# Where the split weights of a three-part network are made: two temporary buffers against the raw tile itself

## The chip, the core and the metric

The kernel runs on one core of one Trainium2 chip, as one program. The metric is the device time of one execution in microseconds (us). Engines: PE (matrix products; PEld its weight loads), DVE (elementwise), ACT (elementwise and activations), POOL, and SP, which here only issues DMA transfers. In the trace every engine takes its instructions in the order of the program text; one that has to wait holds up those that stand behind it on that engine.

## The reference, cut to what matters

```python
ret = scale * (q @ k.T) * decay_mask            # 4 batches, 8 heads, 576 positions, 64 wide
x   = (ret @ v)  rearranged to [2304, 512]
h   = x @ w_in                                  # [2304, 2048]
x   = (h * tanh(softplus(h))) @ w_out           # "mish", back to [2304, 512]
g   = x @ w_gate; val = x @ w_val               # [2304, 1536] each
out = (g / (1 + exp(-g)) * val) @ w2_out        # "silu gate", back to [2304, 512]
```

The five weight matrices (`w_in`, `w_out`, `w_gate`, `w_val`, `w2_out`) arrive as 64-bit floats; q, k, v and the output are fp32.

## The kernel before

**Products in parts.** PE multiplies fp32r words. Each weight and each activation is split into a high part (a rounding copy, on ACT) and a low part (the fp32 word minus its high part, on DVE), and each product is made of three matrix products: high by high, high by low, low by high. A raw weight tile needs conversion first: each 64-bit word lies in it as two 32-bit halves, and `rebias_raw` (L112: an ACT scale, a DVE shift), `sign` (L117) and `join` (L121) turn each pair of halves into one fp32 word. In the kernel before the joined words lie in every second place of the raw tile ("lo"); the places between ("hi") are then free.

**Stages.** (1) Retention, to about 106 us of the trace. (2) `slot(s)` (L728), s = 4 to 63, in four blocks of sixteen: one tile of the hidden layer is made (`g1`, twelve matmuls on `h`, L664), `mish` and the split run on ACT and DVE (L715, L722, L726), and four slots later the tile goes into the four accumulators (`g2`, twelve matmuls on `acc`, L698). When a block of sixteen ends, `g2_out` (L703) copies the accumulators out, two on ACT, two on DVE, and the next block's activations are split (L364 on ACT, L369 on DVE). (3) The last third of the tokens runs by Strassen's scheme, seven products for eight: `pair1(0)` to `pair1(7)` (L954), seven products each (`te`, L883). (4) The second network by the same scheme (`strassen`, L1092, `outs2`, L1195).

**What the scheme needs of the weights.** Of each block of four sub-matrices a11, a12, a21, a22 the products use seven (`USES`, L178): a11, a12, a22 and the sums s1 = a21+a22, s3 = a11-a21, s2 = s1-a11, s4 = a12-s2. They are made once, during stages 2 and 3, stored to DRAM (`comb1`, `comb`, `combf`) and streamed back when wanted. The first network's weights (`group1(i)`, L289, eight groups) lie already split in SBUF; the second network's (`group(n)`, L219, eighteen groups of two raw tiles) are loaded, converted, summed, split and stored. Raw tiles alternate between two sets of two.

**Parts.** `cast` (L195) takes a tile from the pool `c` (two buffers, one tag) and writes the high part of a run of words into it; `lower` (L200) writes the low part beside it and issues one store for each sub-matrix on SP. A group has four such runs (of the plain words one of 512 and one of 256 columns, and two of 512 with the sums, which lie in "hi"), so every buffer is used twice in a group, and a cast waits on ACT until the stores from its buffer have landed.

**Order and pace.** The order is written out by hand. The steps of all groups stand in one list (`pieces`, L331), each with a cost; `Pace` (L340) adds an allowance at the end of every slot or product and runs as many steps as it covers. `third` (the `group1` steps) gets 3.0 in each slot from s = 20, which lasts to s = 31; `second` (the `group` steps) gets 3.1 in each of s = 32 to 50, 2.3 in s = 51 to 63 and 1.03 at each product of `pair1(1)` to `pair1(7)` (L52, L752 to 757, L1009). A group costs 8.25. The load of group n+1 stands behind the first step of group n on SP. Groups 16 and 17 are worked in stage 4 with tiles lent from the weight space (`raw_second`, `parts_second`, L1049, L1055).

Of the kernel before, what the change touches and what calls it, by code (L numbers as in the profile page):

```python
# [7 lines left out]
F32 = mybir.dt.float32  # L8
# [8 lines left out]
def retention_mish_swiglu(  # L17
# [33 lines left out]
    NC = 4  # L51
    RATES, AHEAD = (3.0, 3.1, 2.3, 1.03), 45  # L52
    EARLY = (9, 11, 14, 17)
# [36 lines left out]
    def words(j):  # L90
        w = raw[j].rearrange("p (n t) -> p n t", t=2)
        return w[:, :, 0], w[:, :, 1]
# [93 lines left out]

    def parts_first(nm, n):
        return pools["c"].tile([128, 2, n, KH], F32R, tag="c", name=nm)

# [16 lines left out]

    def put(x, dsts, nm):
        lower(x, cast(x, nm), dsts)
# [5 lines left out]
    def combine(v, names):  # L214
        for o, a, b, op in ADDS:
            if o in names:
                nc.vector.tensor_tensor(out=v[o], in0=v[a], in1=v[b], op=op)

    def group(n):  # L219
        i, z = divmod(n, 2) if n < 2 * PAIRS else (n - 2 * PAIRS, 2)  # L220
        keys = [f"{'gvf'[z]}{i}_{e}" for e in range(2)]
        v = {}

        def load():
            for e in range(2):
                src = rows(w2_out, 2 * i + e) if z == 2 else cols((w2_gate, w2_val)[z], 2 * i + e)
                raw_load(keys[e], src, z == 2, e + 2 * (n % 2))
                lo, hi = words(keys[e])
                for h in range(2):
                    r, k = (h, e) if z == 2 else (e, h)  # L230
                    v[f"a{r + 1}{k + 1}"] = lo[:, h * KH:(h + 1) * KH].bitcast(F32)
                    v["s" + "1324"[2 * e + h]] = hi[:, h * KH:(h + 1) * KH].bitcast(F32)

        def dst(nm):
            c = USES.index(nm)
            if z == 2:
                return combf[c][i // 2][:, i % 2]
            c += z * NG
            return comb[i][c // 2][:, c % 2]

        def runs():
            lo, hi = ([words(k)[w].bitcast(F32) for k in keys] for w in range(2))
            one, two = (0, 1) if z == 2 else (1, 0)
            return [
                (lo[two], ("a12", "a22") if z == 2 else ("a11", "a12")),
                (lo[one][:, :KH] if z == 2 else lo[one][:, KH:], ("a11",) if z == 2 else ("a22",)),
                (hi[0], ("s1", "s3")), (hi[1], ("s2", "s4")),
            ]

        def step(k):  # L250
            x, names = runs()[k]
            c = {}

            def first():
                c[0] = cast(x, f"c{n}_{k}")

            return first, lambda: lower(x, c[0], [dst(nm) for nm in names])

        def parts_of():
            s = [step(k) for k in range(4)]  # L260

            def add_then(nm, f):
                combine(v, (nm,))
                f()

            def both(f, g):
                f()
                g()

            return [  # L270
                lambda: add_then("s1", s[0][0]), s[0][1], lambda: add_then("s3", s[1][0]),
                lambda: both(s[1][1], s[2][0]), lambda: combine(v, ("s2",)), s[2][1],
                lambda: add_then("s4", s[3][0]), lambda: None, s[3][1],
            ]

        found = []

        def nth(k):
            if not found:
                found.extend(parts_of())  # L280
            found[k]()

        return load, [
            (0.55, lambda: rebias_raw(keys[0])), (0.55, lambda: rebias_raw(keys[1])),
            (0.7, lambda: sign(keys[0])), (0.7, lambda: join(keys[0])),
            (0.7, lambda: sign(keys[1])), (0.7, lambda: join(keys[1])),
        ] + [(t, lambda k=k: nth(k)) for k, t in enumerate((0.45, 0.7, 0.45, 0.45, 0.45, 0.7, 0.45, 0.0, 0.7))]

    def group1(i):  # L289
        v = {}  # L290

        def whole():
            x = rp.tile([128, 2 * DM], U32, tag="raw3", name=f"e{i}").bitcast(F32)
            for e in range(2):
                u = unit["in", 2 * i + e]
                for h in range(2):
                    nm = f"a{e + 1}{h + 1}"
                    if nm in USES:
                        m = i * NG + USES.index(nm)
                        nc.sync.dma_start(  # L300
                            out=comb1[m // 2][:, m % 2], in_=u[:, :, h * KH:(h + 1) * KH].bitcast(F32)
                        )
# [5 lines left out]
            v["x"] = x  # L308
            v["s1"], v["s2"], v["s3"], v["s4"] = v["a22"], v["a11"], v["a21"], v["a12"]

        c = {}

        def first(*halves):
            for k in halves:
                c[k] = cast(v["x"][:, k * DM:(k + 1) * DM], f"e{i}_{k}")

        def rest(k):
            at_ = [i * NG + USES.index(nm) for nm in (("s2", "s4"), ("s3", "s1"))[k]]
            lower(v["x"][:, k * DM:(k + 1) * DM], c[k], [comb1[m // 2][:, m % 2] for m in at_])

        def adds(k):
            combine(v, (("s2", "s4"), ("s1", "s3"))[k])
            first(k)

        return [
            (1.4, whole), (0.85, lambda: adds(1)), (0.85, lambda: adds(0)), (0.7, lambda: rest(1)), (0.7, lambda: rest(0)),
        ]
# [329 lines left out]
    with tc.manual_schedule():  # L657
# [221 lines left out]

        def product(p, w, y, begin):  # L880
            for kk in range(KT // 2):
                for a, x in ((0, 0), (0, 1), (1, 0)):
                    nc.tensor.matmul(  # L883
                        p, lhsT=w[:, a, kk * 128:(kk + 1) * 128], rhs=y[kk][:, x, :],
                        start=begin and kk == 0 and (a, x) == (0, 0), stop=kk == KT // 2 - 1 and a == 1,
                        skip_group_check=True,
                    )
# [66 lines left out]
        def pair1(i):  # L954
# [22 lines left out]
            for c, (nm, tn, begin) in enumerate(PRODUCTS):  # L977
# [3 lines left out]
                m = i * NG + c  # L981
                product(p, su["e", m // 2][:, m % 2], ys["e", c], begin)
                if m % 2:
# [68 lines left out]

        turn = [0]

        def parts_second(nm, n):  # L1055
            turn[0] += 1
            return place("out", 13 + turn[0] % 3, [128, 2, n, KH], F32R, nm)

# [33 lines left out]
        def strassen(n, i, z):  # L1092
# [30 lines left out]
            for c, (nm, tn, begin) in enumerate(PRODUCTS):  # L1123
# [3 lines left out]
                m = z * NG + c  # L1127
                product(p, su[n, "gv", i, m // 2][:, m % 2], ys[n, c], begin)
                if m % 2:
# [65 lines left out]
        def outs2(n, work):  # L1195
# [50 lines left out]
            for c, (nm, tn, begin) in enumerate(PRODUCTS):  # L1246
# [8 lines left out]
                for count, (i, m) in enumerate(at_):  # L1255
                    w, g = su[n, "f", c, i // 2][:, i % 2], gt[n, c, i]
                    for a, x in ((0, 0), (0, 1), (1, 0)):
                        nc.tensor.matmul(  # L1258
                            p[m], lhsT=g[:, x, m * 128:(m + 1) * 128], rhs=w[:, a, :],
                            start=begin and i == 0 and (a, x) == (0, 0) and not (shared and m == 1),  # L1260
                            stop=a == 1 and i == PAIRS - 1, skip_group_check=True,
                        )
# [102 lines left out]
```

## Time and profile before

| | us |
|---|---|
| median of three runs (927.26 to 927.62) | 927.3 |
| the profiled execution | 930.68 |
| its span, first to last instruction | 928.6 |
| mean granted TensorE clock of the span | 0.981 of full speed |
| PE busy / DVE busy / ACT busy | 899.0 / 640.5 / 398.4 |
| stage 2 from s = 32 on, and `pair1(0)` | 224.3 to 378.3, 378.3 to about 395 |

The profile is read in three steps: what PE waits for, since PE is busy in 97% of the span; which engine made it wait, and behind what that engine itself stood; and what a stretch without such waits costs. A row of the timeline gives start, duration, engine, line, operation, tiles, and in brackets how long the engine sat idle before it and what ended that. Busy times of PE are pipelined and run into each other, so the pace of PE is read from numbers of matmuls in a stretch.

### The profile page before, as it was taken

The numbers are of one execution on the slowest core, as the hardware profiler recorded it, in microseconds if no ns is written. First come the engines' busy times: TensorE is split into PE (matmuls) and PEld (weight loads), VectorE is DVE, ScalarE is ACT, GpSimd is POOL, SyncE is SP. The second block draws the span as 40 slices with busy tenths as digits, with TensorE's granted clock in tenths as the row PEclk, the third lists the DMA queues.
The fourth block names the chain that finished last, engine by engine and source line by source line (L and its number), as shares of the span: only waits on it lengthen the run. The fifth ranks groups of instructions, "written<-read, shape, count | busy, mean of one in ns | idle before, by whom it ended". The sixth has DMA issues, their size and how long they took to land.

```text
span 928.6 us, 16096 instructions
## 1 busy us (share of the span) xinstructions
PE 899.0 (97%) x6122; PEld 874.6 (94%) x6122; DVE 640.5 (69%) x1233; ACT 398.4 (43%) x803; POOL 52.7 (6%) x47
## 2 busy tenths in 40 slices
PE   9899999999899789899999999999999999999997
PEld 8798999999899789899999999999999999999997
DVE  3678699578666676566768588787558587566772
ACT  3677466334444454444545333245221345222260
POOL 3554200000000000000000000000000000000000
PEclk9799999999999889899999999999999999999999
DMA  9999266099776666768876689977977777977773
GB/s 216 241 249 245 69 184 191 12 305 296 227 233 196 206 215 221 240 209 273 278 246 204 224 275 343 312 239 249 315 252 247 251 243 260 299 252 255 236 248 113
DMA packets 155261, 217.50 MB, mean 234 GB/s; under 512 B 47792, under 2 KB 119216, under 8 KB 155184
## 3 DMA queue, kind: packets, MB, share of 16 engines
q1 hardware_dynamic: 153648, 215.25, 74.3%
q10 hardware_dynamic: 1536, 1.21, 0.4%
q8 instruction: 49, 0.80, 0.4%
q14 instruction: 28, 0.23, 0.1%
HBM read 164.00 MB, written 52.43 MB: 233 GB/s over the span
## 4 chain that ended last, share of the span: by engine, by line
PE 73%; DVE 11%; ACT 7%; DMA 6%; issue 2%; SPq 0%; ACTq 0%; DVEq 0%
PE t L883 24%; PE T L1258 15%; PE ea L921 7%; PE te L883 6%; PE h L664 6%; PE acc L698 5%; DMA comb<-c 3%; PE s L486 2%; PE o L567 2%; PE o L554 1%; ACT g L722 1%; DVE g L726 1%; ACT c L197 1%; ACT m L715 1%; DMA ecomb<-e 1%
## 5 line engine op out<-in xcount | busy, mean ns | idle before, releaser
L883 PE MATMUL t<-y,su 128*128 128x384 f32 x1512 | 268.6, 337 | 2.5 <-DVE u L890 2.0
L883 PEld LDWEIGHTS t<-y,su 128*128 128x128 f32 x1512 | 263.5, 188 | 5.9 <-DVE u L890 3.3
L664 PE MATMUL h<-xs,u 128*128 128x384 f32 x768 | 147.8, 342 | 4.4 <-ACT xs L364 3.2
L698 PE MATMUL acc<-g,u 128*128 128x384 f32 x720 | 137.9, 341 | 9.0 <-ACT y L708 8.6
L664 PEld LDWEIGHTS h<-xs,u 128*128 128x128 f32 x768 | 137.5, 193 | 5.6 <-ACT xs L364 3.5
L698 PEld LDWEIGHTS acc<-g,u 128*128 128x128 f32 x720 | 128.4, 192 | 10.1 <-ACT y L708 9.3
L1258 PE MATMUL T<-su,g 128*128 128x256 f32 x1134 | 135.7, 282 | 0.0
L1258 PEld LDWEIGHTS T<-su,g 128*128 128x128 f32 x1134 | 135.6, 190 | 0.0
L921 PE MATMUL ea<-ge,u 128*128 128x512 f32 (+1 forms) x384 | 76.0, 337 | 0.0
L883 PE MATMUL te<-ye,eu 128*128 128x384 f32 x336 | 69.4, 342 | 4.0 <-ACT scratch L987 4.0
L726 DVE TENSOR_TENSOR g<-m,g 128x384 fp32r<-128x384 f32 x64 | 35.6, 556 | 51.2 <-ACT g L722 50.9
L921 PEld LDWEIGHTS ea<-ge,u 128*128 128x128 f32 x384 | 62.0, 188 | 5.8
L883 PEld LDWEIGHTS te<-ye,eu 128*128 128x128 f32 x336 | 58.1, 192 | 6.3 <-ACT scratch L987 4.3
L1104 ACT ACTIVATE sg<-sg 128x384 f32<-128x384 f32 x54 | 28.4, 525 | 61.1 <-DVE sg L890 61.1
L1067 ACT CAST g<-ga 128x384 fp32r<-128x384 f32 x72 | 32.5, 516 | 44.8 <-DVE ga L1112 31.3
L1133 ACT COPY p<-t 128x384 f32<-128x384 f32 x35 | 16.6, 473 | 80.8 <-PE t L883 80.8
L1060 DVE TENSOR_TENSOR g<-ga,g 128x384 fp32r<-128x384 f32 x72 | 36.2, 550 | 10.5 <-ACT g L1067 10.5
L715 ACT ACTIVATE m<-h 128x384 f32<-128x384 f32 x64 | 31.1, 487 | 25.6 <-PE h L664 25.5
L890 DVE TENSOR_TENSOR u<-t,p 128x384 f32<-128x384 f32 x36 | 20.0, 556 | 27.0 <-PE t L883 25.1
L890 DVE TENSOR_TENSOR v<-t,p 128x384 f32<-128x384 f32 x36 | 20.0, 557 | 22.8 <-PE t L883 22.7
L197 ACT CAST c<-rawg 128x512 fp32r<-128x512 f32 (+1 forms) x24 | 14.4, 599 | 46.5 <-DMA comb<-c 28.5
L722 ACT CAST g<-m 128x384 fp32r<-128x384 f32 x64 | 32.9, 514 | 1.8
(137 smaller groups left out, 1102.2 us busy)
## 6 DMA issues: line engine op xcount, KB each, us to landing
su<-comb SPq DMA_DIRECT2D x126, 512.0 KB, 4.3
su<-fcomb SPq DMA_DIRECT2D x63, 512.0 KB, 4.2
comb<-c SPq DMA_DIRECT2D x84, 256.0 KB, 2.6
eu<-ecomb SPq DMA_DIRECT2D x28, 512.0 KB, 4.7
fcomb<-c SPq DMA_DIRECT2D x42, 256.0 KB, 3.1
raw<-in_moe_w_in_dram SPq DMA_DIRECT2D x16, 512.0 KB, 4.5
raw<-in_moe_w_out_dram SPq DMA_DIRECT2D x16, 512.0 KB, 3.9
ecomb<-e SPq DMA_DIRECT2D x32, 256.0 KB, 3.1
```

The source lines that it names most:

```text
L664: nc.tensor.matmul(ps, lhsT=u[:, a, kk * 128:(kk + 1) * 128], rhs=s[:, e, :], start=(c == 0), stop=(c == n - 1),)
L698: nc.tensor.matmul(accs[b][d][:, :T], lhsT=u[:, a, d * 128:(d + 1) * 128], rhs=g[:, e, :], start=(i == 0 and c == 0), stop=(i == F1 - 1 an ...
L715: nc.scalar.activation(w, hs.pop(s), AF.Mish)
L722: nc.scalar.copy(out=gs[s][:, 0, :], in_=ws[s])
L726: nc.vector.tensor_tensor(out=g[:, 1, :], in0=ws.pop(s), in1=g[:, 0, :].bitcast(F32), op=ALU.subtract)
L883: nc.tensor.matmul(p, lhsT=w[:, a, kk * 128:(kk + 1) * 128], rhs=y[kk][:, x, :], start=begin and kk == 0 and (a, x) == (0, 0), stop=kk == ...
L890: nc.vector.tensor_tensor(out=out_, in0=a, in1=b_, op=ALU.add)
L921: nc.tensor.matmul(o, lhsT=u[:, a, d * 128:(d + 1) * 128], rhs=y[:, :512] if r == 0 else y[:, 512:], start=f == 0 and (a, x) == (0, 0) and ...
L1060: nc.vector.tensor_tensor(out=out_, in0=a, in1=b_, op=ALU.subtract)
L1067: nc.scalar.copy(out=gt[n, c, i][:, 0], in_=x)
L1104: nc.scalar.activation(x, bank_ if part_ is None else x, AF.Silu)
L1258: nc.tensor.matmul(p[m], lhsT=g[:, x, m * 128:(m + 1) * 128], rhs=w[:, a, :], start=begin and i == 0 and (a, x) == (0, 0) and not (shared ...
```

## The change

The high and low parts of the second network's plain sub-matrices are made inside the raw tile; the sums get two tiles of their own; stores go out from there.

- `join_` writes the joined words densely into the front half of the raw tile (it read and wrote every second place before). The back half is then free.
- `cast` no longer takes a tile; it writes the high part of a run into the back half of the raw tile, and `lower` puts the low part over the words in the front. Stores of a11, a12, a22 read the raw tile.
- s1 and s3 are written into tile c0, s2 and s4 into c1 (`sums`), each with room for both parts; these two tiles have one buffer each (pool `c` had two buffers of one tag, the same space). Their high part goes beside them, the low part over them.
- The order of steps in a group is new, its cost 8.7, and the load of group n+1 stands behind its fourth step. The pace at the products of `pair1` is 1.1. In `group1` the sums also go to c0 and c1, and the casts stand one step later.
- In DRAM the second network's parts now lie low first, so `product` and the last product of `outs2` pick the parts by index.

```diff
-    RATES, AHEAD = (3.0, 3.1, 2.3, 1.03), 45
+    RATES, AHEAD = (3.0, 3.1, 2.3, 1.1), 45
...
-    def cast(x, nm):
-        c = parts(nm, x.shape[1] // KH)
-        nc.scalar.copy(out=c[:, 0], in_=x.rearrange("p (n k) -> p n k", k=KH))
-        return c
-    def lower(x, c, dsts):
-        nc.vector.tensor_tensor(
-            out=c[:, 1], in0=x.rearrange("p (n k) -> p n k", k=KH), in1=c[:, 0].bitcast(F32), op=ALU.subtract
-        )
-        for n, dst in enumerate(dsts):
-            nc.sync.dma_start(out=dst, in_=c[:, :, n].bitcast(F32))
+    def cast(hi, x):
+        nc.scalar.copy(out=hi, in_=x.bitcast(F32))
+    def lower(x, hi):
+        nc.vector.tensor_tensor(out=x, in0=x.bitcast(F32), in1=hi.bitcast(F32), op=ALU.subtract)
...
+        def join_(e):
+            lo, hi = words(keys[e])
+            nc.vector.scalar_tensor_tensor(
+                raw[keys[e]][:, :DM], hi, 3, lo, op0=ALU.logical_shift_left, op1=ALU.bitwise_or
+            )
+        def begin(k):
+            sums(v, c, k, 0, f"c{n}_{k}")
+        def lower_two():
+            lower(w[two][:, 0], w[two][:, 1])
+            for h, nm in enumerate(names):
+                out(nm, w[two][:, :, h])
+        def lower_one():
+            lower(w[one][:, 0, own], w[one][:, 1, own])
+            out(only, w[one][:, :, own])
+        def lower_sums(k):
+            lower(c[k][:, 0], c[k][:, 1])
+            for h, nm in enumerate((("s1", "s3"), ("s2", "s4"))[k]):
+                out(nm, c[k][:, :, h])
...
-        ] + [(t, lambda k=k: nth(k)) for k, t in enumerate((0.45, 0.7, 0.45, 0.45, 0.45, 0.7, 0.45, 0.0, 0.7))]
+            (0.45, lambda: both(lambda: begin(0), lambda: cast(w[two][:, 1], w[two][:, 0]), lambda: combine(v, "s1"))),
+            (0.45, lambda: combine(v, "s3")),
+            (0.45, lambda: both(lambda: begin(1), lambda: combine(v, "s2"))),
+            (0.45, lambda: both(lambda: cast(c[0][:, 1], c[0][:, 0]), lambda: combine(v, "s4"))),
+            (0.7, lower_two), (0.7, lambda: lower_sums(0)),
+            (0.45, lambda: both(lambda: cast(c[1][:, 1], c[1][:, 0]), lambda: cast(w[one][:, 1, own], w[one][:, 0, own]))),
+            (0.7, lambda: lower_sums(1)), (0.45, lower_one),
+        ]
...
-        return [
-            (1.4, whole), (0.85, lambda: adds(1)), (0.85, lambda: adds(0)), (0.7, lambda: rest(1)), (0.7, lambda: rest(0)),
-        ]
+        def begin(k):
+            sums(v, c, k, 1, f"e{i}_{k}")
+            for nm in (("s1", "s3"), ("s2", "s4"))[k]:
+                combine(v, nm)
+        def last_cast():
+            cast(c[1][:, 0], c[1][:, 1])
+            rest(0)
+        def sums2():
+            begin(1)
+            cast(c[0][:, 0], c[0][:, 1])
+        return [(1.4, whole), (0.85, lambda: begin(0)), (0.85, sums2), (0.7, last_cast), (0.7, lambda: rest(1))]
...
-            yield steps_[0]
+            yield from steps_[:4]
             if n + 1 < len(gr):
                 yield 0.0, gr[n + 1][0]
-            yield from steps_[1:]
+            yield from steps_[4:]
...
-        pools["c"] = cr.enter_context(tc.tile_pool(name="pc", bufs=2, side="right"))
+        pools["c"] = cr.enter_context(tc.tile_pool(name="pc", bufs=1, side="right"))
```

## Rows read from the trace of the kernel before

**Rows 1.** The page, part 1: busy us, share of the span, instructions
```profile
PE 899.0 (97%) x6122; PEld 874.6 (94%) x6122; DVE 640.5 (69%) x1233; ACT 398.4 (43%) x803; POOL 52.7 (6%) x47
```
**Rows 2.** Waits of PE, 105 to 620 us: total us, times, longest
```profile
PE acc L698 <- ACT y L708: 8.6, 2, 4.5
PE te L883 <- ACT scratch L987: 4.0, 1, 4.0
PE h L664 <- ACT xs L364: 3.2, 1, 3.2
PE h L664 <- DVE xs L369: 1.2, 1, 1.2
```
**Rows 3.** Windows: length, busy us (instructions) by engine, then PEclk, DMA share, GB/s
```profile
160.00:224.30 64.30, 64.30 (x372) 64.30 (x371) 44.01 (x84) 26.21 (x52) 0.00 (x0) 1.00 0.56 182
224.30:378.30 154.00, 140.97 (x771) 139.53 (x769) 106.02 (x214) 74.69 (x149) 0.00 (x0) 0.94 0.70 222
378.30:401.50 23.20, 19.18 (x97) 18.86 (x97) 9.59 (x20) 8.79 (x20) 0.00 (x0) 0.85 0.55 200
401.50:509.50 108.00, 108.00 (x621) 100.97 (x620) 77.39 (x156) 52.68 (x107) 0.00 (x0) 1.00 0.77 251
```
**Rows 4.** Timeline of ACT ahead of the waits of PE, 241 to 386 us
```profile
241.34 0.65 ACT L197 CAST c<-rawg 128x512 fp32r<-128x512 f32 x1 [4.93 <-DMA comb<-c]
241.90 0.48 ACT L715 ACTIVATE m<-h 128x384 f32<-128x384 f32 x1
...
246.86 0.85 ACT L708 COPY y<-acc 128x384 f32<-128x384 f32 x2
...
301.92 0.70 ACT L197 CAST c<-rawv 128x512 fp32r<-128x512 f32 x1 [1.23 <-DVE rawv L123]
...
302.87 0.95 ACT L364 CAST xs<-x 128x384 fp32r<-128x384 f32 x2
...
385.58 0.65 ACT L197 CAST c<-rawg 128x512 fp32r<-128x512 f32 x1 [6.94 <-DMA comb<-c]
```
**Rows 5.** Waits of ACT, 217 to 405 us
```profile
ACT c L197 <- DMA comb<-c: 47.2, 13, 6.9
```
**Rows 6.** Groups of instructions by shape, 231 to 400 us: busy, mean ns | idle before
```profile
L726 DVE TENSOR_TENSOR g<-m,g 128x384 fp32r<-128x384 f32 x32 | 17.8, 556 | 25.3 <-ACT g L722 25.1
L201 DVE TENSOR_TENSOR c<-rawg,c 128x512 fp32r<-128x512 f32 x16 | 11.0, 688 | 9.1 <-ACT c L197 9.1
L123 DVE SCALAR_TENSOR_TENSOR rawg<-rawg 128x512 uint32<-128x512 uint32 x12 | 8.3, 692 | 0.3
L217 DVE TENSOR_TENSOR rawg<-rawg 128x256 f32<-128x256 f32 x11 | 4.6, 421 | 0.1
L115 DVE TENSOR_SCALAR rawg<-rawg 128x512 uint32<-128x512 uint32 x12 | 4.5, 422 | 0.0
```
**Rows 7.** Timeline of DVE and ACT in the `group1` stretch, 179 to 227 us
```profile
179.51 0.89 DVE L217 TENSOR_TENSOR e<-e 128x256 f32<-128x256 f32 x2
...
183.29 1.46 DVE L201 TENSOR_TENSOR e<-e,e 128x512 fp32r<-128x512 f32 x2
184.78 1.29 DVE L304 TENSOR_TENSOR e<-u 128x512 f32<-128x512 f32 x2
...
226.16 1.02 DVE L369 TENSOR_TENSOR xs<-x,xs 128x384 fp32r<-128x384 f32 x2
...
187.84 0.62 ACT L197 CAST e<-e 128x512 fp32r<-128x512 f32 x1 [1.83 <-DMA ecomb<-e]
189.34 0.62 ACT L197 CAST e<-e 128x512 fp32r<-128x512 f32 x1 [0.88 <-DMA ecomb<-e]
```
**Rows 8.** Timeline of PE where s = 32 begins its `g1`
```profile
226.40 4.33 PE L664 MATMUL h<-xs,u 128*128 128x384 f32 x24
```
**Rows 9.** Tiles `rawg`, then `c`: from issue to landing
```profile
DMA to landing us min/median/max: 4.7/5.6/7.2
DMA to landing us min/median/max: 2.0/2.8/6.4
```

More of the change, by code (lines that the diff above doesn't have):

```diff
@@ L185, in raw_first, with parts_first @@
         return rp.tile([128, 2 * DM], U32, tag=f"raw{n}", name=f"raw{key}")
-    def parts_first(nm, n):
-        return pools["c"].tile([128, 2, n, KH], F32R, tag="c", name=nm)
+    def parts_first(k, nm):
+        return pools["c"].tile([128, 2, 2, KH], F32R, tag=f"c{k}", name=nm)
     def raw_load(key, src, whole, n):
@@ L192, in raw_load, with send, combine, sums @@
         nc.sync.dma_start(out=raw[key] if whole else raw[key].rearrange("p (k f) -> p k f", k=KT), in_=src)
-    def cast(x, nm):
-        c = parts(nm, x.shape[1] // KH)
-        nc.scalar.copy(out=c[:, 0], in_=x.rearrange("p (n k) -> p n k", k=KH))
-        return c
-    def lower(x, c, dsts):
-        nc.vector.tensor_tensor(
-            out=c[:, 1], in0=x.rearrange("p (n k) -> p n k", k=KH), in1=c[:, 0].bitcast(F32), op=ALU.subtract
-        )
-        for n, dst in enumerate(dsts):
-            nc.sync.dma_start(out=dst, in_=c[:, :, n].bitcast(F32))
-    def put(x, dsts, nm):
-        lower(x, cast(x, nm), dsts)
+    def cast(hi, x):
+        nc.scalar.copy(out=hi, in_=x.bitcast(F32))
+    def lower(x, hi):
+        nc.vector.tensor_tensor(out=x, in0=x.bitcast(F32), in1=hi.bitcast(F32), op=ALU.subtract)
+    def send(dst, src):
+        nc.sync.dma_start(out=dst, in_=src.bitcast(F32))
     ADDS = (("s1", "a21", "a22", ALU.add), ("s3", "a11", "a21", ALU.subtract),
             ("s2", "s1", "a11", ALU.subtract), ("s4", "a12", "s2", ALU.subtract))
[L214 to L217, printed above, removed]
+    def combine(v, nm):
+        (o, a, b, op), = [x for x in ADDS if x[0] == nm]
+        nc.vector.tensor_tensor(out=v[o].bitcast(F32), in0=v[a].bitcast(F32), in1=v[b].bitcast(F32), op=op)
+    def sums(v, c, k, low, nm):
+        c[k] = parts(k, nm)
+        for n, o in enumerate((("s1", "s3"), ("s2", "s4"))[k]):
+            v[o] = c[k][:, low, n]
     def group(n):
@@ L236, in dst, with out @@
+        def out(nm, src):
+            m = USES.index(nm)
             if z == 2:
[L237 to L243, printed above, removed]
-            return [
-                (lo[two], ("a12", "a22") if z == 2 else ("a11", "a12")),
-                (lo[one][:, :KH] if z == 2 else lo[one][:, KH:], ("a11",) if z == 2 else ("a22",)),
-                (hi[0], ("s1", "s3")), (hi[1], ("s2", "s4")),
-            ]
@@ L250, in step @@
[L250 to L263, printed above, removed]
-                f()
[L266 to L281, printed above, removed]
+                dst = combf[m][i // 2][:, i % 2]
+            else:
+                m += z * NG
+                dst = comb[i][m // 2][:, m % 2]
+            send(dst, src)
+        two, one = (1, 0) if z == 2 else (0, 1)
+        names = ("a12", "a22") if z == 2 else ("a11", "a12")
+        own, only = (0, "a11") if z == 2 else (1, "a22")
+        def join_(e):
[3 more added lines that the diff above has]
+            )
@@ L307, in whole @@
                 )
[L308 to L315, printed above, removed]
-        def rest(k):
[L318 to L325, printed above, removed]
-            (1.4, whole), (0.85, lambda: adds(1)), (0.85, lambda: adds(0)), (0.7, lambda: rest(1)), (0.7, lambda: rest(0)),
-        ]
+        def begin(k):
+            sums(v, c, k, 1, f"e{i}_{k}")
+            for nm in (("s1", "s3"), ("s2", "s4"))[k]:
+                combine(v, nm)
+        def rest(k):
+            lower(c[k][:, 1], c[k][:, 0])
+            for h, nm in enumerate((("s1", "s3"), ("s2", "s4"))[k]):
+                m = i * NG + USES.index(nm)
+                send(comb1[m // 2][:, m % 2], c[k][:, :, h])
+        def last_cast():
[5 more added lines that the diff above has]
+        return [(1.4, whole), (0.85, lambda: begin(0)), (0.85, sums2), (0.7, last_cast), (0.7, lambda: rest(1))]
     FIRST = 4
@@ L878, in retention_mish_swiglu, with product @@
         )
-        def product(p, w, y, begin):
+        def product(p, w, high, y, begin):
             for kk in range(KT // 2):
@@ L1051, in raw_second, with parts_second @@
             return place("in", 9, shape, U32, name) if n % 2 else pools["rx"].tile(shape, U32, tag="rx", name=name)
[L1053 to L1057, printed above, removed]
+        def parts_second(k, nm):
+            return place("out", 13 + k, [128, 2, 2, KH], F32R, nm)
         def sub(out_, a, b_):
```

29 lines of the change are left out of this document (13 added, 16 removed).

## The prediction

> **What bounds the kernel now.** The first view is the busy line of the page: PE is busy in 97% of the span, so only time that PE loses can be won [rows 1]. The second is the list of what PE waited for after retention: four kinds of wait, 17.0 us, nearly all released by ACT [rows 2]. The third asks what these waits cost together, and reads PE's pace by stretch: 372 matmuls in 64.30 us without a wait are 0.173 us each; the 771 of the next stretch should then take 133.3 us and took 154.0, the 97 after them 16.8 and took 23.2 [rows 3]. The loss is 20.7 + 6.4 = 27.1 us. It is more than the 17.0 us of the waits because the granted clock falls to a mean of 0.94 and 0.85 there: after a wait PE runs for a while at half speed, 1.2 instead of 2.4 GHz, which adds 0.6 us to every us waited. The fourth view, the timeline of ACT, tells why ACT was late: ahead of the first wait stands a cast that sat 4.93 us until a store from its buffer had landed, and `mish` and the copies of the accumulators stand behind it; ahead of the last one the same with 6.94 us [rows 4]. Such waits sum to 47.2 us, thirteen of them [rows 5]. Most cost nothing, since a hidden tile is wanted only four slots after its `mish`; those just before a block ends do. From 401.5 us on PE loses next to nothing, so everything that can be won lies between 224 and 401 us.
>
> **The change part by part.**
> *Taken away: the wait of ACT for stores.* In the new order no cast writes a place from which a store of the same group still reads. The back half of a raw tile is free since the load; c0 and c1 are stored once in a group, and their next writer comes ten steps later, at least 5.5 units of cost, 7.4 us at 3.1 units in a slot of 24 x 0.173 = 4.15 us, where a store needs 2.8 us and at most 6.4 [rows 9]. The whole 27.1 us are open to be won; what is late next decides how much of it.
>
> *What is late next in the slots: DVE.* The number of instructions stays: two shifts (0.42), two signs and two joins (0.69), four sums (0.42), three lower parts of 512 columns (0.69) and one of 256 (0.42): 7.8 us in a group, 0.89 us a unit [rows 6]. A slot then takes 3.1 x 0.89 + 0.56 for the low part of `g` = 3.3 us of DVE out of 4.15. So DVE recovers 0.8 us a slot when it is late, and ACT, with less to do, waits for it within a slot (a cast for its sums) without carrying this into the next. At the three block ends and at `pair1(0)`, what PE wants then has 2 us and more of slack if ACT and DVE are on time: copies of the accumulators are wanted 2.1 us after `g2` ends, the split activations 5 us after `g1` ends for some 3 us of work (`mish` 0.48, two copies 0.95, low parts 0.56 each) [rows 4, 6]. The second wait of PE had also a cast behind a join before it, 1.23 us [rows 4]; this is of DVE and stays, within that slack. I put 0.8 us for block ends, between 0 and 6 (two of the old waits back).
>
> *Dense words.* Whether sums and casts read every second word or neighbours: strided sums took 421 ns, dense ones 0.89 us a pair [rows 6, 7]. Nothing.
>
> *Moved: the load of the next group, and the release of raw tiles.* SP isn't paced by slots, so the place behind step four matters little; but the load of the second raw tile now waits until the store of `lower_one` has landed, where it waited for DVE before, and the first stores of the next group and the streams stand behind it on SP. From `lower_one`: 0.5 for the issue, 2.8 for the store, 5.6 for the load, at most 6.4 and 7.2 [rows 9]: 8.9 us, at worst 14. The rebias that wants it stands 9.8 units on, 13.1 us, and ACT reaches it 1 to 2 us ahead of DVE. So it is hidden by 2 us at the medians; without that cover ACT waits at a rebias as it did at a cast. 0.4 us, between 0 and 4. Streams are asked for six tiles ahead and lose nothing.
>
> *`group1`: a new loop through one buffer.* Here the writer of c0 is a sum on DVE, and one buffer is all there is. From the end of a lower part to the cast that its stores held up, the trace has 3.9 and 4.6 us (two lower parts end at 184.0 and 184.75, the casts go at 187.84 and 189.34) [rows 7]. The loop is this, two pairs of sums at 0.89 and a lower part of 0.69: 6.4 to 7.1 us, where the pace asks for a group every 4.5 / 3.0 slots = 6.2 us. So DVE falls behind by 0.1 to 0.8 us a group; it is busy for 44.0 of 64.3 us in this stretch, and part of the waiting falls into that idle time [rows 3]. Followed through s = 20 to 31 with 4.2 us, the low parts of the next block's activations start at 227.7 instead of 226.16 us [rows 7]. PE wants the first seven matmuls into its `g1`, at 226.40 + 7 x 0.173 = 227.6 [rows 8], and gets it at 228.2: 0.6 us lost, with clock 1.0. With 3.9 it is 0, with 4.6 about 4 and with clock 6.4. I take 1.0, as both durations occur and the shorter one held at the first group and later again.
> The Trainium skill, "SBUF — State Buffer", section "The DMA setup-cost knee", gives a transfer about 2 us and its bytes over 436 GB/s: 2.6 us for 256 KB, as an estimate. By it the loop would take 5.7 us, DVE would not fall behind, and the time would be 1.0 us less; the rows above are of this very transfer, with its queue and two stores in a row, and they decide.
>
> *The longer list.* A group costs 8.7 units instead of 8.25 and the slots' allowance stays (88.8), so at 1.1 a product the list ends at (139.2 - 88.8) / 1.1 = the 46th of 49 products instead of the 42nd. From product 45 of `pair1` on (counted from `pair1(0)`) two more instructions of 0.55 run at each product: the two lists overlap for eight products instead of four. DVE then has about 1.0 + 1.1 + 0.6 = 2.7 us in the 2.2 us of a product (108 us for 49) [rows 3] and is late by some 2 to 3 us at the end, just below what the 18 matmuls (3.1 us) between the end of one product and the next into the same accumulator leave. 0.5 us, between 0 and 2. Three products without pieces follow before stage 4, which starts with idle DVE. Groups 16 and 17 keep their places; nothing there.
>
> *The sum.* 27.1 won, less 0.8 + 0.4 + 1.0 + 0.5 = 2.7, net 24.4 us. On the profiled execution: span 928.6 to 904.2, its time 930.68 to 906.3. The median of the runs is 3.4 us below that execution; 927.3 - 24.4 = 903 us. With all costs at 0 it is 900, with all at their upper ends (18.4) 918.6.
>
> **The rivals.**
> *A. As summed:* 903, 900 to 907.
> *B. `group1` runs at the pace of its stores.* With 4.6 us throughout, 6.4 us are lost at s = 32, and the same lateness costs about 2 again at the copies four slots later, with the other costs 1.7: 27.1 - 10.1 = 17.0, 910. For it: 4.6 was seen in the same slot as 3.9. Against: 3.9 is seen too, and PE passes s = 32 today without a wait [rows 8].
> *C. The waits change their name.* ACT stands at the casts of c0 for the sums on DVE, just ahead of a block end, as 1.23 us did at the second wait; half of the loss stays, 13.5 us: 914. Against: DVE has 0.8 us a slot to spare.
> *D. The change doesn't do what it says:* a tile is tracked as a whole, casts into the back half wait for stores of the front, and the 47.2 us of waits return: 927.
> *E. Slower: the raw tile's loop.* Store, load, conversion and `lower_one` of one set of raw tiles run round once in two groups, 2 x 2.81 slots = 23.3 us. By medians the round takes 3.3 + 6.1 + 8.9 (7.8 and two low parts of `g`) = 18.3, by the longest rows 23.5. Above 23.3 the excess goes into ACT's wait at every rebias. To eat 27.1 us in ten groups it has to reach 28.7, that is store and load at nearly twice their medians throughout; then 930 and more. Fourteen stores of 256 KB and four loads of 512 KB in 23.3 us are 250 GB/s; `group1` moves seven such stores in 6.2 us, nearly 300, with stores of 3.9 to 4.6 us, which speaks against it.
>
> **How the numbers follow.** A 0.62, B 0.17, C 0.11, D 0.04, E 0.06. The likeliest is A: 903. From 899 to 913 lie A, B and a third of C, 0.82. A measurement of this kernel can tell about 0.2% from no change: faster 0.90 (A, B, C), the same 0.04 (D), slower 0.06 (E).
>
> **What would show it.** Right: no wait of ACT for a store between 217 and 401 us; the waits of PE for ACT's copies, for its activations and for `pair1(0)` gone, each below 1 us; the granted clock at 1.00 in the slots; about 134 us from s = 32 to `pair1(0)`. Wait rows of DVE for stores in `group1`, about 1 us each, are part of A; beyond 2 us each they speak for B. A rebias that waits for the load of its raw tile speaks for E, casts that wait over 2 us for DVE at a block end for C. I would be wrong if PE finds something else to wait for between 224 and 401 us that today stands in the shadow of ACT.

## The result, and the profile after

The changed kernel takes 899.95 us (median of four, 899.81 to 901.78), the kernel before 927.46 beside it (927.26 to 928.44): the ratio is 0.9706, with an interval of 0.9689 to 0.9723. 903 was forecast. The profiled execution of after took 901.78 us, with a span of 900.0. Two disturbed executions further down, one of `slow_27` (the one with its trace, at a mean granted clock of 0.753) and one of `slow_255`, are counted in the medians and not in the ratios.

The first view is again the page, and now says less than before: PE is busy for 99% where it was 97% [rows 1]. The second row is the granted clock in 40 slices, in tenths.

```profile
PE 888.9 (99%) x6122; PEld 866.5 (96%) x6122; DVE 639.8 (71%) x1233; ACT 396.3 (44%) x803; POOL 52.5 (6%) x47
...
PEclk9799999999999999999999999999999999999999
```

The waits of PE after retention, 105 to 620 us (total us, times, longest), answer to [rows 2]. None of the four kinds is left; what remains sums to 2.0 us, and none of it is for the slots' copies or activations.

```profile
PE t L878 <- DVE u L885: 1.0, 2, 0.6
PE acc L693 <- DVE u L134: 0.3, 1, 0.3
PE o L549 <- DVE x L575: 0.3, 1, 0.3
PE t L878 <- ACT p L1125: 0.2, 1, 0.2
PE t L878 <- DVE v L885: 0.2, 1, 0.2
```

The windows (length, busy us and instructions of PE, PEld, DVE, ACT, POOL, then PEclk, DMA share, GB/s) answer to [rows 3]. The same slots, s = 32 to 63, that took 154.0 us with 771 matmuls now take 133.2 with 768, at clock 1.00; `pair1` follows without a loss.

```profile
160.00:224.30 64.30, 64.30 (x373) 64.30 (x372) 44.59 (x86) 27.63 (x54) 0.00 (x0) 1.00 0.55 177
224.30:357.50 133.20, 133.20 (x768) 133.20 (x768) 101.70 (x204) 71.08 (x145) 0.00 (x0) 1.00 0.79 253
357.50:372.00 14.50, 14.50 (x85) 14.50 (x85) 8.13 (x18) 6.69 (x15) 0.00 (x0) 1.00 0.74 246
372.00:482.00 110.00, 110.00 (x631) 103.05 (x630) 81.24 (x165) 54.15 (x110) 0.00 (x0) 1.00 0.79 257
```

Of the waits of the other engines, 160 to 405 us, three rows matter. The 47.2 us that ACT stood for stores [rows 5] have no row any more. ACT waits for sums on DVE instead, 13.0 us in nine pieces, which costs PE nothing; the sums of `group1` wait for stores, and once a raw tile comes 0.8 us late.

```profile
ACT c L196 <- DVE c L209: 13.0, 9, 3.2
...
DVE e L209 <- DMA ecomb<-e: 10.0, 13, 3.0
...
ACT rawg L114 <- DMA rawg<-in_moe_w_gate_dram: 0.8, 1, 0.8
```

ACT at the end of the first block answers to [rows 4], where a cast sat 4.93 us and the copies of the accumulators went at 246.86. They now go at 241.72, just as PE's `g2` has ended, and PE takes the next `g2` at 243.29 without a wait.

```profile
241.72 0.85 ACT L703 COPY y<-acc 128x384 f32<-128x384 f32 x2
```

### The profile page after: what moved, and what is told of

Its sections match the earlier page's. It is cut to its first block, busy times and chain, and to the rows that moved or that the text cites. A ratio compares the mean times of both kernels' runs of the same rounds, so it can differ in the third digit from the quotient of the medians.

```text
span 900.0 us, 16088 instructions
## 1 busy us (share of the span) xinstructions
PE 888.9 (99%) x6122; PEld 866.5 (96%) x6122; DVE 639.8 (71%) x1233; ACT 396.3 (44%) x803; POOL 52.5 (6%) x47
## 4 chain that ended last, share of the span: by engine, by line
PE 92%; DVE 5%; ACT 1%; DMA 1%; issue 0%; SPq 0%; ACTq 0%; DVEq 0%
PE t L878 25%; PE T L1250 15%; PE h L659 14%; PE acc L693 13%; PE ea L916 7%; PE te L878 7%; PE s L481 2%; PE o L562 2%; PE o L549 2%; PE tk L465 1%; PE acc L891 1%; PE state L525 1%; DMA raw<-in_moe_w_in_dram 1%; PE idle L607 1%; PE tq L434 1%; DVE cv L885 1%
## 5 line engine op out<-in xcount | busy, mean ns | idle before, releaser
L659 PE MATMUL h<-xs,u 128*128 128x384 f32 x768 | 143.8, 336 | 0.0
L693 PE MATMUL acc<-g,u 128*128 128x384 f32 x720 | 134.6, 336 | 0.3 <-DVE u L134 0.3
L659 PEld LDWEIGHTS h<-xs,u 128*128 128x128 f32 x768 | 133.9, 188 | 0.4
L693 PEld LDWEIGHTS acc<-g,u 128*128 128x128 f32 x720 | 125.8, 188 | 0.6 <-DVE u L134 0.6
L721 DVE TENSOR_TENSOR g<-m,g 128x384 fp32r<-128x384 f32 x64 | 35.6, 556 | 47.2 <-ACT g L717 46.8
L1125 ACT COPY p<-t 128x384 f32<-128x384 f32 x35 | 16.5, 473 | 80.7 <-PE t L878 80.7
L885 DVE TENSOR_TENSOR u<-t,p 128x384 f32<-128x384 f32 x36 | 20.0, 556 | 28.3 <-PE t L878 27.2
L196 ACT CAST c<-c 128x512 fp32r<-128x512 f32 x36 | 22.2, 619 | 13.4 <-DVE c L209 13.4
```

Of the source, the lines that this page charges most:

```text
L659: nc.tensor.matmul(ps, lhsT=u[:, a, kk * 128:(kk + 1) * 128], rhs=s[:, e, :], start=(c == 0), stop=(c == n - 1),)
L693: nc.tensor.matmul(accs[b][d][:, :T], lhsT=u[:, a, d * 128:(d + 1) * 128], rhs=g[:, e, :], start=(i == 0 and c == 0), stop=(i == F1 - 1 an ...
L721: nc.vector.tensor_tensor(out=g[:, 1, :], in0=ws.pop(s), in1=g[:, 0, :].bitcast(F32), op=ALU.subtract)
L885: nc.vector.tensor_tensor(out=out_, in0=a, in1=b_, op=ALU.add)
```

## The experiments

Each kernel was run beside the kernel before; a ratio is against that. The theory at first was the prediction's: the gain is the waits of ACT for stores from two rotating buffers, and of these only the ones just ahead of a block end cost anything. Its rivals were the dense words, the new order and pace, and later the pace of before alone.

### Dense words alone

`dense_only` is the kernel before with the joined words in the front half of the raw tile and the sums in its back half; buffers, order and pace are the old ones.

```diff
-            lo, hi = words(keys[e])
+            lo, hi = raw[keys[e]][:, :DM], raw[keys[e]][:, DM:]
...
-            (0.7, lambda: sign(keys[0])), (0.7, lambda: join(keys[0])),
+            (0.7, lambda: sign(keys[0])), (0.7, lambda: join_(0)),
```

> The kernel before with one thing of the change alone: the joined words are written densely into the front half of the raw tile and the sums lie in the back half; parts still go through the two rotating c tiles, in the old order and at the old pace. Theory (ACT's waits for stores from c are the whole gain): ACT still waits some 45 to 50 us for comb stores between 217 and 405 us, PE still loses about 27 us, time 925 to 929 us. Rival (dense words make sums, casts and low parts cheaper, which is what helped): DVE and ACT groups shorter by 50 ns or more each, time below 915 us.

Measured: 926.76 us, ratio 0.9991 (0.9976 to 1.0006). ACT's waits for stores are as before, 47.1 us in twelve, and so are PE's: 6.7, 5.1, 4.2 and 2.0 us. Dense words bring nothing.

### The new order and pace, without working in place

`order_only` is the changed kernel with all four runs of a group through two rotating buffers of one tag again; the order, the cost of a group, the place of the load and the pace are the new ones.

```diff
-            (0.45, lambda: both(lambda: begin(0), lambda: cast(w[two][:, 1], w[two][:, 0]), lambda: combine(v, "s1"))),
+            (0.45, lambda: both(lambda: up("two", w[two][:, 0]), lambda: combine(v, "s1"))),
...
-        pools["c"] = cr.enter_context(tc.tile_pool(name="pc", bufs=1, side="right"))
+        pools["c"] = cr.enter_context(tc.tile_pool(name="pc", bufs=2, side="right"))
```

> The changed kernel with its in-place parts undone: the new order of steps, the new cost of a group, the place of the load, the new pace and the dense words stay, but high and low parts of all four runs go through two rotating c tiles again (one tag, two buffers) and the sums lie in the back half of the raw tiles. Theory: the casts of s2/s4 and of the single sub-matrix must wait for stores issued two steps earlier, so ACT waits 3 to 4 us in each group, 35 to 45 us in all, and PE loses part of it at the block ends: 908 to 930 us. Rival (the new order and pace put the steps where they do no harm): 899 to 903 us whatever ACT waits.

Measured: 930.35 us, ratio 1.0038 (1.0022 to 1.0054). The waits for stores are back under new names (217 to 405 us):

```profile
ACT c_s L196 <- DMA comb<-c_two: 39.6, 10, 5.6
ACT c_one L196 <- DMA comb<-c_s: 12.5, 10, 3.4
```

and PE waits 18.4 us in its six largest kinds (105 to 640 us), for the accumulators, the activations and `pair1(0)` as before. So order and pace alone are not the gain. It needs the writes that no store holds up.

### The load late in the list

`late_load` is the changed kernel with the load of group n+1 behind step 12 of group n instead of step 4. It takes away the cover under which the prediction costed that load at 0.4 us.

```diff
-            yield from steps_[:4]
+            yield from steps_[:12]
```

> The changed kernel with a wait of ACT put back by other means: the load of the next group's raw tiles stands behind the twelfth step of a group instead of the fourth, so that it lands (1.0 us of issue, 5.6 us to landing) after ACT has come to the rebias that needs it, some 3 us after the load could be issued. Theory: ACT waits about 3 us for a load in each of the eleven groups of the slots, 25 to 35 us in all, what stands behind it on ACT is late at block ends, PE waits there and its clock falls after it: 905 to 922 us. Rival (waits on ACT are harmless, the gain came from something else): 899 to 902 us.

Measured: 955.89 us, ratio 1.032 (1.0292 to 1.0348), far above what both expected. Waits of ACT and DVE for one of the two pairs of raw tiles, 160 to 460 us (the other pair: 38.8 and 26.7 us):

```profile
ACT rawv L114 <- DMA rawv<-in_moe_w_val_dram: 41.5, 11, 8.5
...
DVE rawv L115 <- DMA rawv<-in_moe_w_val_dram: 36.4, 11, 6.6
```

The first of them on ACT's timeline:

```profile
246.39 0.69 ACT L114 ACTIVATE rawv<-rawv 128x512 f32<-128x512 f32 x1 [8.53 <-DMA rawv<-in_moe_w_val_dram]
```

I had priced one wait of about 3 us a group. It is some 7 us, on ACT and on DVE for the same tile, since DVE's shift needs it too: store, load, conversion, sums and lower parts run one behind the other, and neither engine can work ahead. The groups start 17.2 us apart (the rebias at 246.39 and, four groups later, at 315.19), where the pace asks for one in 8.7 / 3.1 x 4.15 = 11.6. PE pays at the block ends and at `pair1(0)` (its waits, 105 to 620 us):

```profile
PE te L878 <- ACT scratch L982: 13.9, 3, 12.6
PE h L659 <- ACT xs L359: 11.2, 1, 11.2
PE acc L693 <- ACT y L703: 10.3, 2, 7.6
```

This pointed past the theory: what counts might be how long a group takes through its buffers against what the pace asks for, not where a single wait stands.

### `group1` as before

`old_group1` is the changed kernel with the `group1` of before, whose sums stay in place, in a tile of their own, and whose high and low parts alone use c0 and c1. The cut shows the order of steps only.

```diff
...
-        return [(1.4, whole), (0.85, lambda: begin(0)), (0.85, sums2), (0.7, last_cast), (0.7, lambda: rest(1))]
+        return [
+            (1.4, whole), (0.85, lambda: adds(1)), (0.85, lambda: adds(0)), (0.7, lambda: rest(1)), (0.7, lambda: rest(0)),
+        ]
```

> The changed kernel with the first network's groups (group1) as in the kernel before: sums in place in their own tile, parts through c0 and c1. Theory: nothing of the gain comes from group1, and the waits of DVE for ecomb stores (10.0 us in the changed kernel) cost nothing: they vanish, ACT waits some 3 us for such stores instead, time 899 to 901.5 us. Rival (the loop through c0 costs what the prediction put for it): 1 us or more less than the changed kernel. Rival (group1's new order brings part of the gain): 903 us or more.

Measured: 899.01 us, ratio 0.9697 (0.9681 to 0.9713). The sums no longer wait for stores; the casts on ACT do, 7.8 us in five (160 to 227 us), where 3 us were expected. The time is 0.9 us below that of the changed kernel, and the intervals of the two ratios overlap: it makes no difference that can be measured which engine waits there.

### The pace of the changed kernel

Three kernels change only its allowances: `pace_103` goes back to 1.03 a product in `pair1`; `fast_35` asks for 3.5 and 2.6 units a slot, `fast_42` for 4.2 and 3.2, to find where the new buffers end.

```diff
-    RATES, AHEAD = (3.0, 3.1, 2.3, 1.1), 45
+    RATES, AHEAD = (3.0, 4.2, 3.2, 1.1), 45
```

> The changed kernel with the old pace at the products of pair1, 1.03 instead of 1.1: the list then ends at the 49th of 49 products instead of the 46th, so its last steps run right up to the second network's first products. Theory: DVE has room for either, time 899 to 902 us. Rival (the longer list presses on the products and the faster pace was needed): 903 us or more.

> The changed kernel with more steps in a slot (3.5 and 2.6 units instead of 3.1 and 2.3). By the sum of the prediction DVE then has 3.5 x 0.89 + 0.56 = 3.7 us of work in a slot of 4.15, and two groups take 20.6 us, more than the 18.3 us of the raw tile's loop (store, load, conversion): 899 to 903 us, hardly any wait for a load. If DVE were the next bound already (the prediction's rival C), PE would wait at block ends: 905 us or more.

> The changed kernel with 4.2 and 3.2 units in a slot. DVE would have 4.3 us of work in a slot of 4.15, and two groups would take 17.2 us, less than the 18.3 us of the raw tile's loop. Theory: both limits are passed, so ACT waits at rebias for loads and PE waits at block ends, 903 to 925 us. Against it (the estimates of both limits are too high): 899 to 902 us.

Measured: 900.19 us (ratio 0.973, 0.9705 to 0.9756), 900.05 (0.9724, 0.97 to 0.9748) and 911.97 (0.985, 0.9823 to 0.9876). The windows of the slots, first of `fast_35`:

```profile
224.30:357.50 133.20, 133.12 (x766) 132.51 (x765) 110.03 (x223) 75.82 (x151) 0.00 (x0) 1.00 0.87 278
```

then of `fast_42`:

```profile
224.30:357.50 133.20, 123.76 (x694) 121.75 (x693) 116.97 (x236) 76.10 (x153) 0.00 (x0) 0.97 0.90 289
```

and two waits of ACT in it (160 to 405 us; PE's longest is 4.7 us, for ACT's activations):

```profile
ACT c L196 <- DVE c L209: 26.4, 19, 2.8
ACT rawg L114 <- DMA rawg<-in_moe_w_gate_dram: 7.3, 5, 2.7
```

At 3.5 units a group is asked for every 8.7 / 3.5 x 4.15 = 10.3 us and the groups keep to it (from 248.49 to 299.52 us five start, 10.2 apart). At 4.2 units it would be 8.6; five take 9.9 each (246.35 to 295.98), with DVE busy in 88% of the stretch, and ACT waiting for both DVE and the raw tile. So the new form has a limit between 3.5 and 4.2 units, about 9.9 us a group. The prediction named two, DVE and the loop of the raw tile (18.3 us for two groups); both show here, and no run separates them. The 1.1 a product isn't needed.

### The kernel before, with nothing ahead of the block ends

If only the waits just ahead of a block end cost anything, the kernel before should win most of the gain by keeping weights out of those slots. `held` runs no step in eight slots around the three ends and `pair1(0)`, and asks for more in the others.

```diff
-    RATES, AHEAD = (3.0, 3.1, 2.3, 1.03), 45
+    RATES, AHEAD = (3.0, 3.6, 2.8, 1.25), 45
+    HOLD = (33, 34, 45, 46, 49, 50, 62, 63)
...
-            elif s >= PREP:
+            elif s >= PREP and s not in HOLD:
```

> The kernel before, with its buffers, its order of steps and its waits of ACT for stores, but no step of the second network's groups is run in the two slots ahead of each place where PE waited (s = 33, 34, 45, 46, 49, 50, 62, 63); the other slots run 3.6 and 2.8 units instead of 3.1 and 2.3, a product of pair1 1.25 instead of 1.03. Theory (a wait of ACT costs only where a block ends or pair1 begins before ACT has caught up): ACT still waits 35 to 50 us for stores up to 405 us, PE waits less than 6 us at these places, 902 to 913 us. Rival (every such wait costs PE its share wherever it falls, or the in-place parts help in another way): 919 us or more.

Measured: 921.07 us, ratio 0.9925 (0.9897 to 0.9954). That is 14 us above the middle of the expectation, and in the range of the rival (919 us or more). The waits at s = 36, s = 52 and `pair1(0)` are gone, but at s = 48 ACT is a whole slot late in spite of the two free slots, and PE stands for 4.83 us (its timeline):

```profile
298.71 0.44 PE L665 MATMUL h<-xs,u 128*128 128x384 f32 x1 [4.83 <-ACT xs L365]
```

The starts of three groups on ACT's timeline, in a stretch without a held slot, tell why:

```profile
248.50 1.25 ACT L115 ACTIVATE rawv<-rawv 128x512 f32<-128x512 f32 x2
...
262.58 1.26 ACT L115 ACTIVATE rawg<-rawg 128x512 f32<-128x512 f32 x2
...
275.39 1.27 ACT L115 ACTIVATE rawv<-rawv 128x512 f32<-128x512 f32 x2
```

and the windows show PE without a loss in that stretch (157 x 0.173 = 27.2), a loss of 11.3 us up to 370 (145.7 - 777 x 0.173), and one of 8.3 in `pair1`:

```profile
248.50:275.40 26.90, 26.90 (x157) 26.90 (x156) 16.70 (x33) 11.52 (x24) 0.00 (x0) 1.00 0.67 218
...
224.30:370.00 145.70, 137.70 (x777) 136.24 (x776) 97.40 (x197) 70.76 (x142) 0.00 (x0) 0.98 0.65 211
400.00:500.00 100.00, 95.26 (x530) 87.67 (x529) 73.07 (x152) 50.57 (x101) 0.00 (x0) 0.98 0.81 274
```

3.6 units a slot ask for a group every 8.25 / 3.6 x 4.15 = 9.5 us. Through the two buffers they come 14.1 and 12.8 us apart, and the next (at 287.22) 11.8. ACT falls behind by 2 to 5 us a group and meets the block end late although the two slots ahead of it hold no step: it is still at the steps of s = 44 when PE begins s = 48.

### The kernel before, slower

The new theory says: two buffers let a group through in about 13 us; the kernel before asks for one in 8.25 / 3.1 x 4.15 = 11.0, and PE pays the difference. Six groups of it at 3.1 units took 13.4 us each, from rebias to rebias on ACT's timeline:

```profile
231.32 1.27 ACT L114 ACTIVATE rawg<-rawg 128x512 f32<-128x512 f32 x2
...
311.85 1.27 ACT L114 ACTIVATE rawg<-rawg 128x512 f32<-128x512 f32 x2
```

Then a slower pace should take the loss away, with every wait of ACT for a store still there. The list has to end in time, so the steps go to `pair1`. `slow_before` asks for 2.94, 2.18 and 1.043 (a group in 11.6 us, as in the changed kernel), `slow_27` for 2.7, 2.3 and 1.1 (12.7), `slow_255` for 2.55, 2.1 and 1.18 (13.4).

```diff
-    RATES, AHEAD = (3.0, 3.1, 2.3, 1.03), 45
+    RATES, AHEAD = (3.0, 2.55, 2.1, 1.18), 45
```

> The kernel before with the allowances cut by 8.25 / 8.7 (2.94, 2.18, 1.043), so that a group takes as many slots as in the changed kernel. Theory: the waits of ACT stay at 45 us or more and only shift against the block ends; PE loses between 10 and 35 us, 908 to 935 us. Rival (the slower pace of the list is the gain): 899 to 903 us.

> The kernel before with 2.7 units in a slot instead of 3.1 (2.3 in the last thirteen as before, 1.1 at a product of pair1 so that the list ends in time): a group is then asked for every 12.7 us instead of 11.1. New theory (through two rotating buffers a group takes 12 to 13 us, whatever the pace, so that a faster list makes ACT later from group to group until PE pays at a block end): PE loses 4 to 14 us instead of 27, 904 to 914 us, with ACT still waiting 35 us or more for stores. Old theory (each wait costs where it falls just ahead of a block end): a loss like that of 2.94 units, 915 us or more.

> The same with 2.55 units in a slot (2.1 in the last thirteen, 1.18 at a product of pair1): a group every 13.4 us. New theory: the buffers keep up, ACT is late by one wait at most, PE loses under 8 us, 900 to 908 us, though ACT still waits 30 us or more for stores. Old theory: 912 us or more.

Measured: 918.95 us (ratio 0.9914, 0.9889 to 0.994), 918.91 (0.9904, 0.9878 to 0.9929) and 911.17 (0.9835, 0.9815 to 0.9855). `slow_before`, put on record under the old theory, came out in its range, and the slower list is not the gain (899 to 903 us). The other two are slower than the new theory expected: `slow_27` lies in the range of the old one (915 us or more), `slow_255` between the two. `slow_27` has no trace that can be compared. Those of the other two tell where the time goes. First ACT's wait for stores from 224.3 to 370 us, in the kernel before and then in `slow_255`:

```profile
ACT c L197 <- DMA comb<-c: 38.6, 11, 4.9
ACT c L197 <- DMA comb<-c: 30.4, 9, 5.9
```

then that window in the kernel before, in `slow_before` and in `slow_255` (PE's wait for the copies of the accumulators, 8.6 us in [rows 2], is 0.6 in the last), and `pair1` in `slow_255`:

```profile
224.30:370.00 145.70, 132.67 (x723) 131.23 (x722) 99.99 (x202) 68.61 (x136) 0.00 (x0) 0.94 0.69 222
224.30:370.00 145.70, 134.56 (x747) 132.79 (x746) 98.82 (x200) 70.54 (x139) 0.00 (x0) 0.96 0.69 221
224.30:370.00 145.70, 145.10 (x833) 144.05 (x832) 99.97 (x203) 75.06 (x151) 0.00 (x0) 1.00 0.72 233
400.00:500.00 100.00, 94.71 (x517) 85.16 (x516) 73.61 (x148) 50.30 (x99) 0.00 (x0) 0.98 0.78 261
```

In this window PE loses 145.7 - 723 x 0.173 = 20.6 us in the kernel before, 16.5 in `slow_before` and 1.6 in `slow_255`, while ACT's waits for stores only go from 38.6 to 30.4 us. Six groups take 13.4, 13.6 and 13.7 us each (the rebias of `slow_before` at 227.72 and 309.45, of `slow_255` at 227.91 and 309.81), whether 11.0, 11.6 or 13.4 are asked for. So at the two faster paces the buffers set that time (the groups of the changed kernel keep to 10.2 us where that is asked), and only the last pace leaves room for it. Where a wait stands is not what decides here: in `slow_255` a cast waits 4.49 us just ahead of the copies at the end of a block, and PE stands for 0.41 (ACT's timeline, then PE's):

```profile
305.79 0.65 ACT L197 CAST c<-rawv 128x512 fp32r<-128x512 f32 x1 [4.49 <-DMA comb<-c]
...
307.80 2.47 PE L698 MATMUL acc<-g,u 128*128 128x384 f32 x12 [0.41 <-ACT y L708]
```

What is left is lost later: in `pair1` 517 matmuls take 100 us, 10.6 more than at 0.173. There the reading by rate fails. A group is asked for only every 8.25 / 1.18 x 2.2 = 15.4 us, but one cast of each group still waits 3.6 to 6.7 us for a store, DVE's lower part waits for the cast, and behind it stands the sum that PE wants. Waits of ACT and DVE, 400 to 500 us:

```profile
ACT c L197 <- DMA fcomb<-c: 15.7, 3, 6.3
ACT c L197 <- DMA comb<-c: 12.8, 2, 6.7
DVE c L201 <- ACT c L197: 18.6, 15, 3.5
```

About half of the loss lies before 470 us, where all five waits of PE for DVE's scratch follow such a lower part; these waits sum to 2.1 us, and what else is lost there is not shown. The other half lies in the last products, where the second list runs too: DVE has no gap from 473 to 487 us, and PE waits longest there, on its timeline:

```profile
491.22 2.02 PE L883 MATMUL t<-y,su 128*128 128x384 f32 x6 [2.41 <-DVE scratch L890]
```

None of the three paces gives the old buffers the time of the changed kernel: what is slow enough for them in the slots moves groups to `pair1`, where their waits cost again.

## Why the prediction was right, point by point

*What bounds the kernel, and how much is open.* Right. 27.1 us were put down as open between 224 and 401 us; the medians differ by 27.5, and the windows show no loss in that stretch any more.

*Which waits cost.* The step "Most cost nothing ... those just before a block end do" describes where PE stood, but not what set the loss. `held` took the steps away from the ends and still lost 11.3 us in the slots; `slow_255` kept most of the waits, one of them just ahead of a block end, and lost 1.6 us in the slots. The loss in the slots, 20.7 of the 27.1 us, was a rate: groups through two buffers take about 13 us, 11.0 were asked for, and since ACT's order also holds `mish` and the copies, ACT is late by more with each group until PE meets it at a block end. At `pair1(0)`, the other 6.4 us, the step was right: the 2.3 units of the last slots ask for a group in 8.25 / 2.3 x 4.15 = 14.9 us, the last groups start 15.9 and 16.3 apart (340.40, 356.28 and 372.62 us), and the loss comes from where the cast of 6.94 us stands. All this didn't spoil the number, as the change takes away all waits of that kind. It would have misled anyone who wanted to win the time by moving steps in the slots.

*What is late next.* DVE was put at 3.3 of 4.15 us in a slot, 79%; it is busy for 101.7 of 133.2 us, 76%. Costs of 2.7 us were taken off the gain, and about none of them is there; the measured time is that of the sum with all costs at 0 (900), at the lower end of what rival A allowed:

- Block ends: 0.8 forecast, none measured; PE waits for no copy or activation of the slots.
- Load of the next group: 0.4 forecast. SP does wait for the store of the raw tile, as foreseen (224 to 372 us, below); ACT felt it once, 0.8 us, PE never. The cover was rightly named, its price was not: without it the cost is 56 us (`late_load`, 955.89 against 899.95), since the wait sits on ACT and DVE at once.

```profile
SPq L192 <- DMA comb<-rawg: 11.3, 5, 2.7
SPq L192 <- DMA comb<-rawv: 9.6, 4, 2.7
```

- `group1`: 1.0 forecast, none measured. This is the term whose size was wrong. DVE's rows of one group, 196 to 203 us:

```profile
196.56 1.46 DVE L199 TENSOR_TENSOR e<-e 128x512 fp32r<-128x512 f32 x2
...
200.35 0.76 DVE L209 TENSOR_TENSOR e<-e 128x256 f32<-128x256 f32 x2 [0.65 <-DMA ecomb<-e]
201.89 0.89 DVE L209 TENSOR_TENSOR e<-e,e 128x256 f32<-128x256 f32 x2 [0.77 <-DMA ecomb<-e]
202.69 1.46 DVE L199 TENSOR_TENSOR e<-e 128x512 fp32r<-128x512 f32 x2
...
224.92 1.02 DVE L364 TENSOR_TENSOR xs<-x,xs 128x384 fp32r<-128x384 f32 x2
```

The lower parts of c0 and c1 end at 197.28 and 198.0, their buffers are free again at 200.35 and 201.89: after 3.1 and 3.9 us, where the prediction took 3.9 to 4.6 from the first group [rows 7]. The loop through c0 is then two pairs of sums, a lower part and 3.1, 5.6 us; that through c1, whose buffer comes free later, is 6.1 (its lower parts end at 198.0 and 204.15). Both are below the 6.2 that the pace asks for, the second only just, and DVE is not late: the low parts of the next activations go at 224.92, not at 227.7, and even earlier than before. The Trainium skill's "SBUF — State Buffer", section "The DMA setup-cost knee", which the prediction set aside in favour of that row, gave 2.6 us for such a transfer as an estimate: the 3.1 us of c0 lie between the two, the 3.9 of c1 don't. The loop that the prediction makes of this estimate, 5.7 us, doesn't come out of its terms: 2 x 0.89 + 0.69 + 2.6 is 5.1. What the row lacked was that the first group is not like the others: in this run too its buffers are free only after 4.3 and 4.9 us, and SP needs 2.96 us there for the four stores, later 1.97.

```profile
184.05 2.96 SPq L202 DMA_DIRECT2D ecomb<-e  x4
...
197.28 1.97 SPq L202 DMA_DIRECT2D ecomb<-e  x4
```

- The longer list: 0.5 forecast, none measured. DVE does run without a gap from 459.81 to 481 us, as foreseen, but PE waits for nothing there, and `pace_103`, where by the prediction's sum the list ends three products later still, takes the same time.

*The rivals.* B (`group1` at the pace of its stores) fell with the 3.1 us; `old_group1` shows that nothing is lost there. One of the thirteen waits of DVE passed the 2 us that were named as a sign of B: 2.97 us at 228.91, in the last group, behind the low parts that PE wants, and PE lost nothing by it. C (the waits change their name to DVE) is seen in kind, 13.0 us of ACT's waits, without a price at 3.1 units; at 4.2 units it comes true, together with E, at 12 us. D (a tile tracked as a whole) has no row. E (the raw tile's loop) doesn't limit at 3.1 units, and shows at 4.2; `late_load` is what E would have been.

*What stays open.* `slow_before` loses 16.5 us in the slots and 2.9 in `pair1` (561 matmuls from 400 to 500 us). Of `slow_27`, which asks for a group in 12.7 us, only the time is known: some 18 us above the changed kernel, more than the new theory allows, and where they are lost is not shown. What the 13 us or so of a group are made of was measured, not worked out. A third buffer of the old form was not tried.

## What to carry to other kernels

A sum of waits on an engine doesn't tell what they cost. Where its results are wanted only some slots later, as in stage 2 here, ask for the rate: compare the time that one group takes through its buffers with the time between two groups that the order of the work asks for. If the first is longer, moving the waits away from the places where it shows wins little. To test such a reading, slow the producer: if most of the waits stay and the loss goes, it was the rate. Where another engine wants the result at once, as in `pair1`, a single wait can cost although the rate fits. When a space that is already held (here the raw tile's own back half) can take the result, the loop through the buffer goes away instead of being tuned.

## What the runs showed of the hardware that was not expected

- *A wait of PE costs more than its length.* After 4.08 us of waiting at 247.39 in the kernel before, 12 matmuls took 3.60 us where the same 12 take 2.24 later (PE's timeline below). The granted clock of the first stretch was 0.61, so most of it ran at 1.2 GHz, and 1.00 in the second. In sum 17.0 us of waits cost 27.1.

```profile
247.39 3.60 PE L698 MATMUL acc<-g,u 128*128 128x384 f32 x12 [4.08 <-ACT y L708]
...
253.25 2.24 PE L698 MATMUL acc<-g,u 128*128 128x384 f32 x12
```

- *Issuing is not of one price.* In the changed kernel the same four stores took SP 2.96 us in the first group of the `group1` stretch and 1.97 in the third, and a buffer whose stores stand second in the queue is free 0.8 us later than the first (3.9 against 3.1 us).
- *Every second word costs DVE's sums no more than neighbours, and ACT's casts a little.* 256 columns of strided sums took 421 ns [rows 6], of dense ones 417 to 425 ns in the changed kernel. A cast of 512 columns took 657 to 663 ns strided in the kernel before and 620 dense in `dense_only`, whose time can't be told from that of the kernel before.
